# Attention's value products kept in order and side by side, and two 64-row instructions of block 0 widened to 128 rows

## The chip, the cores and the metric

One core of one Trainium2 chip runs the whole program. TensorE (PE in the profile) does the matmuls and transposes, VectorE (DVE) the reductions and part of the copies, ScalarE (ACT) the exponentials and the other copies, GpSimd (POOL) the scaling of probabilities and some subtractions; SyncE (SP) issues the transfers. Each engine runs its instructions in one fixed order and waits on semaphores of the others. The metric is the device time of one execution in microseconds: median 2144.94 of three runs (2144.15 to 2150.67).

## The reference

Attention with a memory read is computed for 4 batches and 8 heads of 576 positions and 64 features, and two feed-forward layers follow. Only attention is touched here.

```python
scores = scale * np.matmul(q, k.transpose(0, 1, 3, 2))
scores = np.where(causal, -1000000000.0, scores)
scores = scores - scores.max(-1, keepdims=True)
a = np.exp(scores)
a /= a.sum(-1, keepdims=True) + 1e-09
local = np.matmul(a, v)
q_p = phi(q)                       # phi(x) = max(x, 0) + exp(min(x, 0))
mem_ret = np.einsum('bhsd,bhde->bhse', q_p, M_prev)
mem_norm = np.einsum('bhsd,bhd->bhs', q_p, z_prev)[..., None] + 1e-06
g = 1.0 / (1.0 + np.exp(-beta))[None, :, None, None]
return (g * mem_ret / mem_norm + (1 - g) * local).astype(np.float32)
```

The result goes through a gated layer (`moe1` in the kernel) and a layer of eight weighted experts (`moe2`).

## The kernel before

Two heads are handled together as a pair; there are 16 pairs. The 576 queries of a head are cut into a first block of 64 (block 0) and four blocks of 128 (blocks 1 to 4). Each pair goes through step sequences, written as Python generators, whose letters stand in three tables (`BEGIN`, `ORDER`, `END`): L loads and splits the inputs, Q prepares phi(q) and its normalizer, S makes the scores and their exponentials, N and K scale the probabilities, V transposes them, W and U multiply them with the values. `ORDER` is one iteration; it is repeated 13 times, each letter taken from the pair that `LAG` gives, so that steps of four neighbouring pairs are interleaved. A scheduler may still move instructions of different steps against each other on each engine; the outcome is a fixed order per engine.

Scores (`scores`, lines 335 to 394). Score tiles `ps` lie in two PSUM buffers that are handed round in turn: block 4 takes both, one for each head (L349, mask L354), then block 3 takes the first one again (L303, 128 x 448), block 2 the second, block 1 the first, block 0 the second (L489, mask L387). A buffer comes free when the exponentials that read it are done: L359 for block 4, one activation for each head, L379 for blocks 3 to 1, L391 for block 0. The exponential needs the row maximum from VectorE first (L358, L375, L389). `QH` and `QL` (L258, L260) are the split queries of a later pair; they have two buffers as well, so `QH` is written when block 0's products (L489, 64 columns), the last to read that buffer, are done.

Transposes (`transposed`, lines 407 to 443). The transposed phi (L414) and probabilities (L424, L432, L441, and L433 for block 0's phi) go to tiles `pt`, three PSUM buffers in turn, and are copied by ScalarE or VectorE into `F`, `T`, `Z` (L398, L403).

Values (`values`, lines 445 to 466). For a pair the output tile `po` collects the memory product (L489, `F`), then for k from 3 to 0 the products of the transposed probabilities `T` with the values (L457): 128, 256, 384 and 512 columns, once for each head. The two heads write the upper and the lower 64 partitions of `po`, so each of these products uses one half of TensorE's columns (the form 128\*64 in the profile, 128\*128 for a full-size instruction and 64\*128 for one that contracts over 64 rows). Every product of plain float32 values is two instructions.

After the 16 pairs `moe1` begins; its weights are unpacked on VectorE (`narrow`, L502 to L507) while its first products run.

Of the kernel before, what the change touches and what calls it, by code (L numbers as in the profile page):

```python
# [12 lines left out]
BF16 = mybir.dt.bfloat16  # L13
# [6 lines left out]
P = 128  # L20
# [20 lines left out]


ORDER = """
    S V L L S Q U V S U V U Q V K U S V S V Q V Q W W V W Q N L V N S V L N V
"""
LAG = {"L": 1, "Q": 0, "S": 0, "N": 0, "K": -1, "V": -1, "W": -1, "U": -2}

# [76 lines left out]
class Kernel:  # L124
# [29 lines left out]

    n_pairs = None

    def attention(self, after=None):
        nc, tc = self.nc, self.tc  # L160
        with ExitStack() as st, ExitStack() as first:
            pool = lambda n, b, to=st, **k: to.enter_context(tc.tile_pool(name=n, bufs=b, reuse_waits="tile", **k))

            self.s1, self.s2 = (pool(f"s{n}", n, first, side="right") for n in (1, 2))
            self.a1, self.a2, self.a3, self.a4 = (pool(f"a{n}", n) for n in (1, 2, 3, 4))
            self.pss = pool("pss", 2, space=PSUM)
            self.pst = pool("pst", 3, space=PSUM)
            self.pso = pool("pso", 1, space=PSUM)
            a1 = self.a1
            self.identb = self.s1.tile([P, P], BF16, name="identb")  # L170
            nc.vector.tensor_copy(self.identb, self.ident)

            self.mask = self.s1.tile([P, P], BF16, name="mask")
            nc.gpsimd.memset(self.mask, 0.0)
            nc.gpsimd.affine_select(
                out=self.mask, in_=self.mask, compare_op=ALU.is_ge, fill=MASKED,
                base=0, pattern=[[1, P]], channel_multiplier=-1,
            )
            self.mask0 = self.s1.tile([64, 2, 64], BF16, name="mask0")
            for j in range(2):  # L180
                nc.vector.tensor_copy(self.mask0[:, j], self.mask[0:64, 0:64])
            busy = self.pso.tile([P, 512], F32, name="po")

            bt = self.s1.tile([P, H], F32, name="bt")
            nc.sync.dma_start(bt, self.beta.partition_broadcast(P))

            eb = self.eb = self.s1.tile([P, H], F32, name="eb")
            nc.scalar.activation(eb, bt, AF.Exp, scale=-1.0)
            nc.vector.tensor_scalar_add(eb, eb, 1.0)
            g1 = self.s1.tile([P, H], F32, name="g1")  # L190
            nc.vector.reciprocal(g1, eb)
            nc.vector.tensor_scalar(g1, g1, -1.0, 1.0, op0=ALU.mult, op1=ALU.add)
            nc.vector.reciprocal(g1, g1)


            self.gs = a1.tile([P, NP, 9], F32, name="gs")
            gv = g1.rearrange("p (a h) -> p a h", h=2)
            for j in range(2):
                nc.vector.tensor_copy(self.gs[64 * j:64 * j + 64, :, 0], gv[64 * j:64 * j + 64, :, j])
                for i in range(4):  # L200
                    nc.vector.tensor_copy(self.gs[:, :, 1 + 2 * i + j], gv[:, :, j])
            wg = self.s1.tile([P, NK, E], F32, name="wg")
            nc.sync.dma_start(wg, self.wg)
            nc.scalar.copy(self.wgs[:, :, 0], wg)
            nc.vector.tensor_sub(self.wgs[:, :, 1], wg, f32(self.wgs[:, :, 0]))

            self.P0 = []
            for n in range(2):
                t = a1.tile([P, 2, D], F32, name=f"P0{n}")
                nc.vector.memset(t, 0.0)  # L210
                self.P0.append(t)

            pairs = [(b, hp) for b in range(B) for hp in range(NP)][:self.n_pairs]
            n = len(pairs)
            live = [dict(b=b, hp=hp, P0=self.P0[hp % 2]) for b, hp in pairs]
            for p in live:
                p["steps"] = {
                    "L": self.load(p), "Q": self.prepare(p), "S": self.scores(p), "N": self.normalize(p),
                    "V": self.transposed(p), "W": self.values(p),
                }  # L220
                p["steps"]["U"], p["steps"]["K"] = p["steps"]["W"], p["steps"]["N"]
            done = object()
            steps = schedule(n)
            for nth, (step, at) in enumerate(steps):
                if nth == len(steps) - len(END.split()) and after:
                    self.ahead = self.load_units()
                    next(self.ahead)
                if step == "X":
                    for _ in range(at):
                        nc.tensor.matmul(busy[:, 0:P], self.mask, self.mask, start=True, stop=True)  # L230
                else:
                    next(live[at]["steps"][step], done)
            first.close()
            if after:
                self.open_early(after)

                with tc.issue_after(self.last_exp.ins):
                    for _ in range(2):
                        next(self.ahead)
                    self.xs = self.split_x(*CHUNKS1[0])  # L240
# [94 lines left out]
    def scores(self, s):  # L335
# [48 lines left out]
        ps = self.pss.tile([P, 2, 512], F32, name="ps")  # L384
        o = ps[:, 0, 0:64]
        self.product(o, cut(q, every, slice(0, P)), cut(k, every, slice(S, S + 64)), True, False)
        nc.tensor.matmul(o, self.mask0.rearrange("k j q -> k (j q)"), self.identb[0:64, 0:64], start=False, stop=True)  # L387
        nm = self.s2.tile([P, 1], F32, name="nm0")
        nc.vector.tensor_reduce(nm, o, axis=AX.X, op=ALU.max, negate=True)  # L389
        for j, h in enumerate(HALVES):  # L390
# [16 lines left out]
    def transposed(self, s):  # L407
        nc, a1, a2 = self.nc, self.a1, self.a2
        phi = s["phi"]

        s["F0"] = F0 = a2.tile([P, 64], F32, name="F0")
        pt = self.pst.tile([P, 512], F32, name="pt")
        for t in range(1, 5):
            nc.tensor.transpose(pt[:, (t - 1) * P:t * P], phi[:, t].rearrange("p j d -> p (j d)"), self.ident)  # L414
        s["F"] = self.split(a2, "F", pt)
        yield

        s["T"] = [self.a4.tile([P, 4, 512], F32, name="T") for j in range(2)]
        for i in range(4, 0, -1):
            for j in range(2):  # L420
                pt = self.pst.tile([P, 512], F32, name="pt")
                for k in range(i):
                    o = (i - 1 - k) * P if j == 0 else 64 + k * P
                    nc.tensor.transpose(pt[:, k * P:(k + 1) * P], s["P"][i][:, j, o:o + P], self.ident)  # L424
                self.copy(
                    8 - 2 * i + j, s["T"][j][:, 0:i, (i - 1) * P:i * P], pt[:, 0:i * P].rearrange("p (k q) -> p k q", k=i)
                )
                yield

        s["Z0"] = Z0 = a1.tile([P, 64], F32, name="Z0")  # L430
        pt = self.pst.tile([P, 512], F32, name="pt")
        nc.tensor.transpose(pt[:, 0:P], s["P0"].rearrange("p j k -> p (j k)"), self.ident)  # L432
        nc.tensor.transpose(pt[:, P:P + 64], phi[0:64, 0].rearrange("p j d -> p (j d)"), self.ident[0:64, 0:64])  # L433
        for h in HALVES:
            self.copy(8, Z0[h], pt[h, h])
        self.copy(8, F0, pt[:, P:P + 64])
        yield
        pt = self.pst.tile([P, 512], F32, name="pt")
        for i in range(1, 5):
            Pi, w = s["P"][i].rearrange("p j k -> p (j k)"), 64 + P * i  # L440
            nc.tensor.transpose(pt[:, (i - 1) * P:i * P], Pi[:, w - 64:w + 64], self.ident)  # L441
        s["Z"] = self.split(a2, "Z", pt)
        yield

    def values(self, s):

        mm, b, T = self.nc.tensor.matmul, s["b"], s["T"]
        x = self.x[:, s["hp"]]
        V0, M = (s["v0m"][:, n * P:n * P + P] for n in range(2))
        po = self.pso.tile([P, 512], F32, name="po")  # L450
        self.product(po, s["MS"], s["F"], True, False)
        yield
        for k in range(3, -1, -1):

            for j, h in enumerate(HALVES):
                v = s["v"][:, 2 * D * k + D * j:2 * D * k + D * j + D]
                mm(po[h, k * P:], v, T[j][:, k, k * P:], start=False, stop=False)  # L457
            yield
        p0 = self.pst.tile([P, 512], F32, name="pt")
        mm(p0[:, 0:64], M, s["F0"], start=True, stop=False)  # L460
        mm(p0[:, 0:64], V0, s["Z0"], start=False, stop=True)
        self.copy(9, x[:, b * S:b * S + 64], p0[:, 0:64])
        yield
        self.product(po, s["V0S"], s["Z"], False, True)
        self.copy(10, x[:, b * S + 64:(b + 1) * S], po)
        yield
# [1025 lines left out]
```

## Time and profile before

| | |
|---|---|
| time of the profiled execution | 2145.09 us |
| its span, first to last instruction | 2143.0 us |
| median of three runs | 2144.94 us |
| TensorE busy, share of the span | 2099.1 us, 98% |
| VectorE, ScalarE, GpSimd busy | 1711.3, 982.6, 530.4 us |
| attention | from the start to about 254 us |
| mean granted TensorE clock | 0.996 |

The profiled execution lies 0.15 us above the median; 2.1 us of it are outside the span. Times in the rows are microseconds from the start of the span. A row of the timeline gives the start, the time until the last of its instructions ends, the engine, the source line, the operation and what it writes and reads; matmuls overlap, so the time that one takes from the engine is read from start to next start. In brackets stands how long the engine sat idle before it and whom it waited for. Rows of windows give the busy time and the number of instructions of each engine, the granted TensorE clock (1.00 is 2.4 GHz, 0.50 is 1.2 GHz) and the transfer rate.

### The profile page before, as it was taken

The page shows a single profiled execution, that of the slowest core. Times are in us where ns is not written, and L with a number is a line of the kernel's source. Part 1 is how long each engine was busy: PE and PEld are TensorE (multiplying, and loading weights), DVE is VectorE, ACT ScalarE, POOL GpSimd, SP SyncE. Part 2 cuts the span into 40 slices and gives each one's busy share as a digit, 9 for nine tenths or more (in the row PEclk, how much of TensorE's full clock was granted, in tenths as well). Part 3 has the DMA queues.
Part 4 walks back from the last instruction along what each step waited for, and adds up shares of the span by engine and source line. Part 5 has one row for each costly group of instructions (what it writes and reads, how often), then busy time and mean ns, then how long its engine had stood idle before and what let it go on. Part 6 is the DMA issues. An engine that isn't in the chain of part 4 may idle for free.

```text
span 2143.0 us, 40649 instructions
## 1 busy us (share of the span) xinstructions
PE 2099.1 (98%) x15848; PEld 1913.9 (89%) x15848; DVE 1711.3 (80%) x3195; ACT 982.6 (46%) x1944; POOL 530.4 (25%) x463
## 2 busy tenths in 40 slices
PE   7999998999999999999999999999999999999999
PEld 5666686878879789999999999999999999999998
DVE  8877798685553676898888889888898888898887
ACT  6888733344332423444444444444444444444442
POOL 7666665000020042121221212212212122121210
PEclk9999999999999999999999999999999999999999
DMA  6322288357567846475565664756647566475564
GB/s 215 126 88 91 91 297 280 136 198 246 191 220 270 284 158 216 160 242 195 192 229 166 236 214 160 246 169 235 213 151 256 182 222 212 160 245 194 194 207 158
DMA packets 123358, 425.76 MB, mean 199 GB/s; under 512 B 13600, under 2 KB 13600, under 8 KB 120096
## 3 DMA queue, kind: packets, MB, share of 16 engines
q1 hardware_dynamic: 123168, 423.17, 58.5%
q8 instruction: 126, 2.06, 0.4%
q14 instruction: 64, 0.52, 0.1%
HBM read 374.36 MB, written 48.76 MB: 197 GB/s over the span
## 4 chain that ended last, share of the span: by engine, by line
PE 75%; DVE 15%; DMA 5%; issue 2%; POOL 2%; ACT 1%; SPq 0%; POOLq 0%; DVEq 0%; ACTq 0%
PE pu L1312 14%; PE pc L1149 13%; PE pq L1312 10%; PE pt L1149 9%; PE po L489 6%; PE pt L1235 4%; PE p L489 4%; DMA xr<-xp 3%; PE pc L489 3%; DVE m L1165 2%; DVE xacc L1318 2%; PE pt L489 2%; PE po L457 2%; PE pq L489 2%; PE pt L424 2%
## 5 line engine op out<-in xcount | busy, mean ns | idle before, releaser
L1312 PE MATMUL pu<-xl,h 128*128 128x256 f32 x3240 | 424.8, 278 | 3.1 <-DVE xacc L1318 2.7
L1149 PE MATMUL pc<-xr,w 128*128 128x256 f32 x3072 | 394.1, 277 | 6.3 <-DMA xr<-xp 4.3
L1312 PEld LDWEIGHTS pu<-xl,h 128*128 128x128 f32 x3240 | 393.1, 188 | 7.6 <-DVE xacc L1318 4.4
L1149 PEld LDWEIGHTS pc<-xr,w 128*128 128x128 f32 x3072 | 370.2, 188 | 9.9 <-issue 5.7
L1312 PE MATMUL pq<-xl,h 128*128 128x256 f32 x2430 | 317.0, 277 | 0.0
L1149 PE MATMUL pt<-xr,w 128*128 128x256 f32 x2304 | 295.0, 277 | 0.1
L1312 PEld LDWEIGHTS pq<-xl,h 128*128 128x128 f32 x2430 | 294.0, 188 | 0.3
L1133 ACT CAST h<-m 128x512 fp32r<-128x512 f32 (+1 forms) x345 | 190.4, 556 | 201.3 <-DVE m L1165 193.6
L1149 PEld LDWEIGHTS pt<-xr,w 128*128 128x128 f32 x2304 | 277.9, 188 | 0.9 <-issue 0.2
L1318 DVE SCALAR_TENSOR_TENSOR xacc<-pu,Pw,xacc 128x256 f32<-128x256 f32 x540 | 237.0, 475 | 39.0 <-PE pu L1312 38.9
L1156 ACT COPY m<-pc 128x512 f32<-128x512 f32 x192 | 111.9, 583 | 252.2 <-PE pc L1149 248.6
L1318 DVE SCALAR_TENSOR_TENSOR xacc<-pq,Pw,xacc 128x256 f32<-128x256 f32 x405 | 177.4, 474 | 47.0 <-PE pq L1312 47.0
L1134 DVE TENSOR_TENSOR h<-m,h 128x512 fp32r<-128x512 f32 (+1 forms) x345 | 207.3, 625 | 1.5
L1055 POOL TENSOR_TENSOR ws<-raw 128x512 f32<-128x512 f32 x62 | 83.7, 1361 | 502.8 <-DMA raw<-w 220.2
L1130 ACT ACTIVATE h<-m 128x512 fp32r<-128x512 f32 x192 | 121.4, 632 | 170.4 <-DVE m L1161 169.3
L1165 DVE SCALAR_TENSOR_TENSOR m<-m 128x512 f32<-128x512 f32 x240 | 186.1, 775 | 14.6 <-ACT m L1192 10.9
L489 PE MATMUL p<-xs,gw 128*128 128x512 f32 (+1 forms) x864 | 173.5, 358 | 6.3 <-DVE hf L674 4.0
L1161 DVE TENSOR_TENSOR m<-pt,m 128x512 f32<-128x512 f32 x192 | 131.2, 683 | 54.1 <-ACT m L1156 52.8
L489 PEld LDWEIGHTS p<-xs,gw 128*128 128x128 f32 x864 | 144.8, 191 | 32.9 <-DVE hf L674 5.6
L1131 DVE SCALAR_TENSOR_TENSOR h<-m,h 128x512 fp32r<-128x512 f32 x192 | 149.1, 777 | 13.0 <-ACT h L1130 12.8
L1042 POOL TENSOR_TENSOR w<-raw,w 128x512 fp32r<-128x512 f32 x17 | 42.1, 2477 | 432.0 <-ACT w L1041 432.0
L489 PE MATMUL po<-h,ws 128*128 128x512 f32 x576 | 144.5, 392 | 2.4 <-ACT h L693 1.2
(244 smaller groups left out, 3015.7 us busy)
## 6 DMA issues: line engine op xcount, KB each, us to landing
xr<-xp SPq DMA_DIRECT2D x480, 512.0 KB, 4.2
raw<-w SPq DMA_DIRECT2D x64, 512.0 KB, 7.4
gw<-kg SPq DMA_DIRECT2D x24, 1024.0 KB, 6.8
graw<-gvo SPq DMA_DIRECT2D x36, 512.0 KB, 5.0
xp<-xl SPq DMA_DIRECT2D x30, 512.0 KB, 4.1
kg<-gw SPq DMA_DIRECT2D x24, 512.0 KB, 4.0
ws<-ko SPq DMA_DIRECT2D x24, 512.0 KB, 3.9
qk<-qkv SPq DMA_DIRECT2D x16, 640.0 KB, 4.2
```

The costliest lines, as they stand in the source:

```text
L489: self.nc.tensor.matmul(out, lhs[a], rhs[b], start=start and n == 0, stop=stop and n == 2, skip_group_check=shared)
L1130: nc.scalar.activation(hi, src, AF.Relu)
L1131: self.later(1, lambda: nc.vector.scalar_tensor_tensor(lo, src, 0.0, f32(hi), op0=ALU.max, op1=ALU.subtract))
L1133: nc.scalar.copy(hi, src)
L1134: self.later(1, lambda: nc.vector.tensor_sub(lo, src, f32(hi)))
L1149: self.marks[3] = nc.tensor.matmul(out[:, j * HT:(j + 1) * HT], w[:, a, j, k], x[:, b, k], start=start and j + k + n == 0, stop=k + n == 3 ...
L1156: self.marks[1] = nc.scalar.copy(t, src)
L1161: nc.vector.tensor_add(t, a, b)
L1165: relu = lambda out, a, b, op: nc.vector.scalar_tensor_tensor(out, a, 0.0, b, op0=ALU.max, op1=op)
L1235: nc.tensor.matmul(ph[:, j * HT:(j + 1) * HT], w[:, b, j, k], x[:, c, k], start=j + a + k + m == 0, stop=a + k + m == 4, skip_group_check= ...
L1312: nc.tensor.matmul(po[:, c], h[a][:, x, j, c * P:(c + 1) * P], w2[b][:, y, j], start=start and c + j + n == 0, stop=j + n == 3, skip_group ...
L1318: self.marks[2] = nc.vector.scalar_tensor_tensor(acc, po[:, c], self.Pw[:, at, e:e + 1], acc, op0=ALU.mult, op1=ALU.add)
```

## The change

The value products of both heads for one k are kept next to each other, and the order in which attention's steps reach TensorE is held: every instruction of a step that is written after a value product is also issued after it on TensorE. In `ORDER` two letters are moved, so that the products for k = 1 and k = 0 stand together, and those for k = 3 and k = 2. Block 0's mask is stored with 128 rows (the lower half zero), and block 0's phi is transposed with 128 rows; both instructions used 64 rows before.

```diff
 ORDER = """
-    S V L L S Q U V S U V U Q V K U S V S V Q V Q W W V W Q N L V N S V L N V
+    S V L L S Q V S U U V U Q V K U S V S V Q V Q W W W V Q N L V N S V L N V
 """
...
-    n_pairs = None
+    n_pairs = last_value = None
...
-            self.mask0 = self.s1.tile([64, 2, 64], BF16, name="mask0")
+            self.mask0 = self.s1.tile([P, 2, 64], BF16, name="mask0")
+            nc.gpsimd.memset(self.mask0, 0.0)
             for j in range(2):
-                nc.vector.tensor_copy(self.mask0[:, j], self.mask[0:64, 0:64])
+                nc.vector.tensor_copy(self.mask0[0:64, j], self.mask[0:64, 0:64])
...
-                    next(live[at]["steps"][step], done)
+                    with ExitStack() as order:
+                        if self.last_value:
+                            order.enter_context(tc.issue_after(self.last_value.ins))
+                        next(live[at]["steps"][step], done)
...
-        nc.tensor.matmul(o, self.mask0.rearrange("k j q -> k (j q)"), self.identb[0:64, 0:64], start=False, stop=True)
+        nc.tensor.matmul(o, self.mask0.rearrange("k j q -> k (j q)"), self.identb[:, 0:64], start=False, stop=True)
...
-        nc.tensor.transpose(pt[:, P:P + 64], phi[0:64, 0].rearrange("p j d -> p (j d)"), self.ident[0:64, 0:64])
+        nc.tensor.transpose(pt[:, P:2 * P], phi[:, 0].rearrange("p j d -> p (j d)"), self.ident)
...
-                mm(po[h, k * P:], v, T[j][:, k, k * P:], start=False, stop=False)
+                self.last_value = mm(po[h, k * P:], v, T[j][:, k, k * P:], start=False, stop=False)
+                self.tc.keep_in_program_order(self.last_value)
```

In the changed file these lines are 4 to 5 further down: the value products L457 are L461 there, the transposes L424 are L428, the products L303, L349 and L489 are L307, L353 and L494, the exponentials L359 are L363, `QH` is L262.

On TensorE, in the middle of one iteration of the steady part, the order before is this (`ps` scores, `pt` transposes, `po` output; L457 with "x2" is both heads, without it one head):

```order
L414 MATMUL pt<-ident,ph 128x128 x4
L457 MATMUL po<-T,vm 64x384 x2
L424 MATMUL pt<-ident,P_1576 128x128 x4
L457 MATMUL po<-T,vm 64x512
L303 MATMUL ps<-KH,QH 128x448 x2
L303 MATMUL ps<-KL,QH 128x448 x2
L303 MATMUL ps<-KH,QL 128x448 x2
L373 LDWEIGHTS mask
L373 MATMUL ps<-identb,mask 128x128
L373 LDWEIGHTS mask
L373 MATMUL ps<-identb,mask 128x128
L457 MATMUL po<-T,vm 64x512
```

And in the changed kernel, at the same place on TensorE:

```order
L418 MATMUL pt<-ident,ph 128x128 x4
L428 MATMUL pt<-ident,P_1577 128x128 x4
L307 MATMUL ps<-KH,QH 128x448 x2
L307 MATMUL ps<-KL,QH 128x448 x2
L307 MATMUL ps<-KH,QL 128x448 x2
L377 LDWEIGHTS mask
L377 MATMUL ps<-identb,mask 128x128
L377 LDWEIGHTS mask
L377 MATMUL ps<-identb,mask 128x128
L461 MATMUL po<-T,vm 64x384 x2
L461 MATMUL po<-T,vm 64x512 x2
```

The 384-column products and one head's 512-column product have moved from ahead of block 3's scores (128x448) to behind them.

At the end of the same iteration TensorE's order before is:

```order
L489 MATMUL po<-F,vmr 128x512 x3
L457 MATMUL po<-T,vm 64x128 x2
L424 MATMUL pt<-ident,P_1700 128x128
L457 MATMUL po<-T,vm 64x256 x2
L424 MATMUL pt<-ident,P_1700 128x128
L489 MATMUL ps<-KH,QH 128x64
```

In the changed kernel TensorE has there:

```order
L494 MATMUL po<-F,vmr 128x512 x3
L461 MATMUL po<-T,vm 64x128 x2
L461 MATMUL po<-T,vm 64x256 x2
L428 MATMUL pt<-ident,P_1701 128x128 x2
L494 MATMUL ps<-KH,QH 128x64
```

One transpose no longer stands between the 128- and the 256-column products.

On ScalarE, from the split of the queries to the exponentials of block 4, the order before is:

```order
L258 ACTIVATE QH<-qk 128x640
L391 ACTIVATE P_176,sums<-ps,nm_1744 64x64 x2
L398 COPY Z_1748<-pt 64x64 x2
L398 COPY F_1596<-pt 128x64
L403 CAST Z<-pt 128x512
L280 ACTIVATE ph<-zq 128x640
L264 CAST KH<-qk 128x640
L403 CAST F<-pt 128x512
L359 ACTIVATE P_1775,sums<-ps,nm_1792 128x576
```

In the changed kernel ScalarE's order over the same stretch is:

```order
L262 ACTIVATE QH<-qk 128x640
L395 ACTIVATE P_177,sums<-ps,nm_1745 64x64 x2
L402 COPY Z_1749<-pt 64x64 x2
L402 COPY F_1597<-pt 128x64
L407 CAST Z<-pt 128x512
L284 ACTIVATE ph<-zq 128x640
L268 CAST KH<-qk 128x640
L407 CAST F<-pt 128x512
L363 ACTIVATE P_1776,sums<-ps,nm_1793 128x576
```

Nothing has moved in this stretch of ScalarE.

## Rows read from the trace of the kernel before

**Rows 1.** Windows, the steady part of attention: busy time by engine, clock, transfers

```profile
80.00:222.00 142.00, 142.00 (x972) 87.39 (x971) 104.75 (x220) 120.82 (x347) 88.41 (x138) 1.00 0.28 89
```

**Rows 2.** Timeline of TensorE, one iteration of the steady part

```profile
150.02 0.44 PE L457 MATMUL po<-T,vm 128*64 128x128 f32 x4
150.39 0.33 PE L424 MATMUL pt<-ident,P 128*128 128x128 f32 x1
150.65 0.65 PE L457 MATMUL po<-T,vm 128*64 128x256 f32 x4
151.23 0.33 PE L424 MATMUL pt<-ident,P 128*128 128x128 f32 x1
...
151.54 0.28 PE L489 MATMUL ps<-KH,QL 128*128 128x64 f32 x1
...
152.34 0.66 PE L441 MATMUL pt<-ident,P 128*128 128x128 f32 x4
...
154.89 0.87 PE L457 MATMUL po<-T,vm 128*64 128x384 f32 x4
155.69 0.66 PE L424 MATMUL pt<-ident,P 128*128 128x128 f32 x4
156.28 1.07 PE L457 MATMUL po<-T,vm 128*64 128x512 f32 x2
157.28 0.47 PE L303 MATMUL ps<-KH,QH 64*128 64x448 f32 x2
...
158.30 1.07 PE L457 MATMUL po<-T,vm 128*64 128x512 f32 x2
159.30 0.66 PE L424 MATMUL pt<-ident,P 128*128 128x128 f32 x4
...
164.38 0.44 PE L457 MATMUL po<-T,vm 128*64 128x128 f32 x4
```

**Rows 3.** Timeline of ScalarE in the same iteration

```profile
151.74 0.74 ACT L258 ACTIVATE QH<-qk 128x640 fp32r<-128x640 f32 x1 [0.72 <-PE ps L489]
...
156.12 0.74 ACT L359 ACTIVATE P<-ps,nm 128x576 f32<-128x576 f32 x1
```

**Rows 4.** Timeline of ScalarE and of TensorE at the start of attention

```profile
15.62 0.74 ACT L359 ACTIVATE P<-ps,nm 128x576 f32<-128x576 f32 x1 [2.73 <-DVE nm L358]
...
16.51 0.47 PE L303 MATMUL ps<-KH,QH 64*128 64x448 f32 x2 [2.38 <-ACT P L359]
```

**Rows 5.** Timeline of TensorE at the end of attention, last pair

```profile
251.12 1.72 PE L457 MATMUL po<-T,vm 128*64 128x384 f32 x8
252.77 0.43 PE L460 MATMUL pt<-F,vm 128*128 128x64 f32 x2
```

**Rows 6.** Timeline of ScalarE, third pair and fifth

```profile
42.87 0.74 ACT L359 ACTIVATE P<-ps,nm 128x576 f32<-128x576 f32 x1
...
79.93 0.74 ACT L258 ACTIVATE QH<-qk 128x640 fp32r<-128x640 f32 x1 [0.25 <-PE ps L489]
```

**Rows 7.** Timeline of TensorE, three waits at and after the end of attention

```profile
245.96 0.74 PE L424 MATMUL pt<-ident,P 128*128 128x128 f32 x5 [2.80 <-DVE xacc L398]
...
340.27 3.02 PE L489 MATMUL p<-xs,gw 128*128 128x512 f32 x12 [2.17 <-DVE sg L674]
...
365.50 10.08 PE L489 MATMUL p<-xs,gw 128*128 128x512 f32 x36 [1.92 <-DVE hf L674]
```

**Rows 8.** Windows behind those waits

```profile
246.00:249.00 3.00, 3.00 (x17) 2.30 (x19) 2.67 (x6) 2.19 (x5) 1.28 (x1) 0.66 0.16 18
249.00:252.00 3.00, 3.00 (x17) 1.34 (x15) 2.06 (x5) 2.01 (x7) 1.94 (x1) 0.77 0.62 244
340.00:360.00 20.00, 19.11 (x81) 15.16 (x82) 19.34 (x34) 8.37 (x15) 8.21 (x5) 1.00 0.83 265
360.00:370.00 10.00, 8.08 (x29) 6.17 (x28) 8.57 (x16) 2.77 (x5) 5.15 (x3) 0.83 0.79 280
```

**Rows 9.** Timeline of TensorE, value products of the last pair in the first of these windows

```profile
248.21 1.55 PE L457 MATMUL po<-T,vm 128*64 128x128 f32 x8
```

## The prediction

> **What bounds the kernel now.** I read the windows of attention first, because the change touches nothing else. Between 80 and 222 us TensorE is busy all the time, ScalarE 120.82 of 142.00 us, VectorE 104.75 and GpSimd 88.41 [rows 1]. That looks like a stage that any relief of TensorE shortens. The timeline then gives one iteration: from one 128-column value product to the next are 164.38 - 150.02 = 14.36 us [rows 2]. Last I looked for the places where TensorE and ScalarE meet, since ScalarE has only some 2.1 us of slack in an iteration (14.36 x 21.18 / 142). Two matter. ScalarE waits 0.72 us before it splits the queries (`QH`, 151.74), for the last product of block 0 that reads the buffer (151.54, row of TensorE) [rows 2, 3]. And TensorE may begin block 3's scores (157.28) only when the first exponential of block 4 (156.12) has freed the score buffer [rows 2, 3]. Where TensorE truly waited for that exponential, its product started 16.51 - 15.62 = 0.89 us after the exponential's start [rows 4]. So at 157.28 the buffer had been free since 156.12 + 0.89 = 157.01: in the steady part that limit is hidden by 0.27 us only. Behind it stands what TensorE does before it, above all the 384-column products and one head's 512-column product.
>
> **The change part by part, TensorE's own work.** A block of value products costs 0.37 us for 128 columns, 0.58 for 256 and 0.80 for 384, both heads together (150.02 to 150.39, 150.65 to 151.23, 154.89 to 155.69) [rows 2]: 0.21 for 128 more columns and about 0.16 for entering and leaving the half-width form. One head's 512 columns alone cost 1.00, and that twice (156.28, 158.30) [rows 2]. 384 and 512 columns of both heads in one block cost 252.77 - 251.12 = 1.65 us [rows 5]. So 0.80 + 1.00 + 1.00 = 2.80 becomes 1.65, and 0.37 + 0.58 = 0.95 becomes 0.79. The transpose between the two small blocks (0.26, 150.39 to 150.65) falls to the pitch of a run, about 0.09; the four transposes behind the 384 columns (0.59, 155.69 to 156.28) lose some 0.1. Block 0's last product, its mask, a transpose and the 64-row transpose take 152.34 - 151.54 = 0.80 now [rows 2]; in one form the four are estimated at 0.4. Together TensorE loses 1.15 + 0.16 + 0.17 + 0.1 + 0.4 = 2.0 us of work in an iteration.
>
> The Trainium skill (TensorEngine Tiling (Array Packing), Tiling Modes, key properties) says that different tiles of the array compute in parallel and that a change of the tiling mode drains it. The trace agrees: two heads' 384 columns take less than one head's 512, and each separate block pays its 0.16 [rows 2]. By that rule alone 13 iterations would give the gain that stands below as the second rival.
>
> **Where the time of an iteration goes then.** In the order of the changed kernel the following chain closes on itself, whatever TensorE has to spare. From `QH` to the first exponential of block 4 ScalarE does the same instructions in the same order as before, without a hole: 156.12 - 151.74 = 4.38 [rows 3]. Then 0.89 to block 3's first product [rows 4], 1.02 to the end of its mask (157.28 to 158.30), the joint block 1.65 [rows 5], the unchanged stretch to the 128-column products, 164.38 - 159.30 = 5.08, from there to block 0's last product 151.54 - 150.02 = 1.52 less 0.16 and 0.17, so 1.19, and 0.20 to the next `QH` [rows 2, 3]. The sum is 14.41 us against 14.36. What was taken from TensorE ahead of block 3's scores is lost there as a wait, and the value products put behind them (1.65 where 1.00 stood) lengthen the chain by what the other end saves. TensorE would reach block 3's scores at about 154.89 + 0.59 - 0.4 = 155.1, and the buffer is free at 157.01: a new wait of some 1.9 us on ScalarE in each iteration. Queued behind it are the value products, the second half of block 4's transposes and the copies of ScalarE that need them. I count 10 such iterations: 10 x 0.05 = +0.5 us. Bounds: -0.1 to +0.2 for each, if the estimated pitch of the transposes or the exponential's release is off by a tenth.
>
> The early pairs. The third pair's exponential starts at 42.87, held by VectorE [rows 6], which unpacks weights there; it is not moved. With the changed order block 3 follows at 42.87 + 0.89 = 43.76, the next `QH` 1.02 + 1.65 + 5.08 + 1.19 + 0.20 = 9.14 later at 52.9, and two more iterations of 14.41 bring it to 81.7, where it stood at 79.93 [rows 6]: +1.8. VectorE has its unpacking between block 3's maximum and block 2's in the new order, which may add up to 1.0. I take +2.3, with bounds of 0 (the unpacking moves out of the way) and +3.
>
> The last pairs keep TensorE's order except for block 0's two widened instructions and the joint small block; ScalarE's copies there wait for block 0's transposes, so about 0.4 is gained: -0.4, bounds -1 and 0.
>
> The memset of the mask on GpSimd and the pins themselves cost nothing: GpSimd waits for the first inputs then, and a pin only fixes the order, which is counted above. The feed-forward layers keep their work; the shift of attention's end passes through to the end, give or take 2 us for the unpacking of weights on VectorE.
>
> **The clock.** TensorE had no idle time in the steady part [rows 1] and the clock held 1.00, its level of 2.4 GHz. A wait of 1.9 us is new. This trace shows what can follow one: after idle 2.80 us (until 245.96) the granted clock of the next stretches is 0.66 and 0.77, a time at the level of 1.2 GHz within them; after 1.92 us (until 365.50) it is 0.83; after 2.17 us (until 340.27) it stays 1.00 [rows 7, 8]. So I expect about half of the 13 waits (third pair to the thirteenth iteration) to be followed by a time at half clock. Its price: 128 and 256 columns together, 0.79 at full clock, took 1.48 there by the start of the next instruction (1.55 to the end) [rows 9], and over both windows 3.00 x 0.34 + 3.00 x 0.23 = 1.7 us of clock are missing [rows 8]. What follows the wait lies on the closed chain with no slack, so nearly all of it counts: I take 1.3 each, 6.5 x 1.3 = +8.5, bounds 0 and 13 x 1.7 = +22.
>
> The Trainium skill (TensorE: Matmul & The Clock Gate, Why this matters for your kernels) advises against idle gaps only when they are longer than this one; by it the clock would hold and the sum would be the first rival's. The trace speaks against it with the wait of 1.92 us [rows 7, 8], and for it with the one of 2.17.
>
> **Sum.** 0.5 + 2.3 - 0.4 + 8.5 = +10.9 us on the profiled execution's 2145.09, which lies 0.15 above the median: 2156 us.
>
> **The rivals.** First, the clock holds: the same closed chain, without the 8.5: 2145.09 + 2.4 = 2147.5, no change that counts. For it speaks the wait of 2.17 us without a fall; against it the other two. Chance 0.28.
>
> Second, not slower but faster: TensorE alone sets the pace, as its 142.00 of 142.00 suggest [rows 1]. Then 13 x 2.0 = 26 us go, to about 2119. Its place is block 3's scores: it decides if the first exponential of block 4 comes 1.9 us sooner after `QH`. Against it: ScalarE's stretch has neither a hole nor a new order. Chance 0.05.
>
> Third, every wait costs the clock, at 1.7: 2145.09 + 2.4 + 22 = 2169.6. For it speaks that most waits of this size in the trace did. Chance 0.10.
>
> Fourth, the layers behind attention take the shift back: TensorE waits for VectorE's unpacked weights there, two of these waits alone 2.17 and 1.92 us [rows 7]; if VectorE gets ahead, some 5 of the 10.9 us return: 2151. Chance 0.08.
>
> That the change does not do what it says: the order shows both heads side by side, but if two heads gained nothing from it the block of 1.65 would be about 3.5 and the time above 2170. The rows exclude nearly all of this; 0.02. The forecast keeps 0.47.
>
> **How the numbers follow.** A measurement of this kernel tells about 0.3%, 6.4 us, from no change: 2138.5 to 2151.4 counts as the same. Slower takes most of the forecast (0.44 of 0.47), the third rival, part of the fourth and the last: 0.58. The same takes the first rival, part of the fourth and what is left of the forecast: 0.36. Faster is the second rival and a little more for the early pairs: 0.06. The range of 8 in 10 runs from 2145, which takes in the first rival, to 2167, which leaves out most of the third. The forecast's own range is 2150 to 2163.
>
> **What would show it.** Right: in the steady part an idle time of TensorE before block 3's scores, put down to the exponential L363, of 1.5 to 2.2 us in nearly every iteration; a period of 14.3 to 14.5 us where the clock is full and about 1.3 longer where it fell; granted clock below 1.00 in several windows of 80 to 222 us; value products of both heads in one block of 1.65 us. Wrong: a period near 12.5 us, no idle time of TensorE there, or a clock of 1.00 throughout.

## The result, and the profile after

The changed kernel took 2157.1 us (median of 5 runs, 2155.0 to 2162.6) against 2144.9 before (5 runs): 1.0057 times, 95% interval 1.0042 to 1.0072. Predicted were 2156 us. The profiled execution is the longest of the five, 2162.6 us with a span of 2160.8; what is read from it below adds up to more than the 12.2 us between the medians.

The windows of the profile show the same stretch as [rows 1]: the window, its length, busy time of TensorE, its weight loads, VectorE, ScalarE and GpSimd, the granted clock, transfers.

```profile
80.00:222.00 142.00, 127.57 (x923) 86.91 (x922) 95.12 (x208) 115.98 (x326) 83.72 (x130) 0.95 0.30 96
```

TensorE, busy all of the 142 us before, now idles 14.4 of them, and the clock fell from 1.00 to 0.95. The table of waits for that stretch has a single entry for TensorE (total, times, longest):

```profile
PE ps L307 <- ACT P L363: 14.4, 9, 1.6
```

Nine waits of 1.6 us at block 3's scores, each for block 4's first exponential. ScalarE's timeline, to be held against [rows 3]:

```profile
87.14 0.27 ACT L402 COPY T<-pt 128x128 f32<-128x128 f32 x1 [0.48 <-PE pt L428]
87.39 0.74 ACT L262 ACTIVATE QH<-qk 128x640 fp32r<-128x640 f32 x1
...
88.45 0.31 ACT L395 ACTIVATE P<-ps,nm 64x64 f32<-64x64 f32 x1
...
91.77 0.74 ACT L363 ACTIVATE P<-ps,nm 128x576 f32<-128x576 f32 x1
...
101.82 0.75 ACT L262 ACTIVATE QH<-qk 128x640 fp32r<-128x640 f32 x1
```

QH to the exponential is 4.38 us as before, and QH to QH 14.43 us where it was 14.36. TensorE in the same iteration, and at the start of block 3 of the next:

```profile
87.19 0.28 PE L494 MATMUL ps<-KH,QL 128*128 128x64 f32 x1
...
88.90 0.40 PE L353 MATMUL ps<-KH,QH 64*128 64x288 f32 x1
...
90.01 0.61 PE L418 MATMUL pt<-ident,ph 128*128 128x128 f32 x4
90.46 0.60 PE L428 MATMUL pt<-ident,P 128*128 128x128 f32 x4
92.66 0.47 PE L307 MATMUL ps<-KH,QH 64*128 64x448 f32 x2 [1.60 <-ACT P L363]
...
93.68 1.72 PE L461 MATMUL po<-T,vm 128*64 128x384 f32 x8
95.33 0.66 PE L428 MATMUL pt<-ident,P 128*128 128x128 f32 x4
...
107.09 0.47 PE L307 MATMUL ps<-KH,QH 64*128 64x448 f32 x2 [1.59 <-ACT P L363]
...
108.11 2.76 PE L461 MATMUL po<-T,vm 128*64 128x384 f32 x8
110.79 1.11 PE L428 MATMUL pt<-ident,P 128*128 128x128 f32 x4
```

The joint block takes 95.33 - 93.68 = 1.65 us, as [rows 5] said. After the wait that ends at 107.09 the same eight products take 2.68 us, behind an equal wait at 92.66 they don't. The windows behind three of the waits, as [rows 8]:

```profile
92.00:96.00 4.00, 3.34 (x23) 1.75 (x23) 2.62 (x5) 2.52 (x7) 1.64 (x2) 1.00 0.33 75
106.00:110.00 4.00, 2.91 (x16) 1.18 (x16) 2.62 (x4) 2.86 (x7) 2.06 (x3) 0.83 0.24 44
...
166.00:170.00 4.00, 3.53 (x14) 1.57 (x16) 2.62 (x4) 2.52 (x7) 1.44 (x1) 0.59 0.38 105
```

From the wait that ends at 60.59 on there are 12 such waits; half clock (1.2 GHz) follows 6 of them (60.59, 76.6, 107.09, 166.5, 182.5, 213.0). An iteration with a fall lasts 16.06 us (101.82 to 117.88), 1.63 more than one without. Only this execution of the five has a trace, so how many falls the median one had isn't known.

The early pairs lost most in one place, between the fourth QH (34.34) and the fifth (55.33), 20.99 us apart where 14.93 stood. TensorE's waits there, and the windows behind the first:

```profile
37.00 1.12 PE L428 MATMUL pt<-ident,P 128*128 128x128 f32 x4 [2.62 <-POOL P L337]
...
43.73 0.74 PE L307 MATMUL ps<-KH,QH 64*128 64x448 f32 x2 [2.20 <-ACT P L363]
```

```profile
38.00:42.00 4.00, 2.96 (x15) 2.30 (x14) 4.00 (x7) 3.60 (x12) 2.88 (x2) 0.50 0.16 23
42.00:46.00 4.00, 2.27 (x10) 1.26 (x12) 3.89 (x8) 1.67 (x4) 3.54 (x7) 0.50 0.57 210
```

Some 10 us are at half clock; what that stretch cost is read at the end of the experiments. The later QH of [rows 6] stands at 87.39 instead of 79.93, +7.5, and the last one at 223.75 instead of 209.19, +14.6. (Called the fifth in the rows' heading and in two expectations, it is the seventh of sixteen; here it is "the QH of [rows 6]".)

### The profile page after: what moved, and what is told of

Its sections match the earlier page's. It is cut to its first block, busy times and chain, and to the rows that moved or that the text cites. A ratio compares the mean times of both kernels' runs of the same rounds, so it can differ in the third digit from the quotient of the medians.

```text
span 2160.8 us, 40647 instructions
## 1 busy us (share of the span) xinstructions
PE 2092.6 (97%) x15848; PEld 1920.8 (89%) x15848; DVE 1709.3 (79%) x3195; ACT 985.3 (46%) x1944; POOL 527.2 (24%) x464
## 4 chain that ended last, share of the span: by engine, by line
PE 76%; DVE 11%; DMA 5%; POOL 3%; issue 2%; ACT 2%; SPq 0%; POOLq 0%; ACTq 0%; DVEq 0%
PE pu L1317 15%; PE pc L1154 13%; PE pq L1317 10%; PE pt L1154 10%; PE po L494 6%; PE pt L1240 4%; PE p L494 4%; DMA xr<-xp 3%; PE pc L494 3%; PE pt L494 2%; PE pq L494 2%; PE po L461 2%; POOL na L523 2%; DVE xacc L1323 2%; DVE m L1170 2%
## 5 line engine op out<-in xcount | busy, mean ns | idle before, releaser
L494 PE MATMUL p<-xs,gw 128*128 128x512 f32 (+1 forms) x864 | 170.9, 354 | 5.1 <-DVE sg L679 2.2
L494 PEld LDWEIGHTS p<-xs,gw 128*128 128x128 f32 x864 | 142.4, 188 | 31.9 <-DVE sg L679 3.5
L494 PE MATMUL po<-h,ws 128*128 128x512 f32 x576 | 146.0, 395 | 2.7 <-ACT h L698 1.5
```

What stands on the lines that cost most here:

```text
L494: self.nc.tensor.matmul(out, lhs[a], rhs[b], start=start and n == 0, stop=stop and n == 2, skip_group_check=shared)
```

## The experiments

Each was timed beside the kernel before on the same chip, whose median was 2146.0 us for experiments 1, 2 and 4, 2144.0 for 3, 5 and 6, and 2145.4 for 7. Ratios are to it. The changed kernel was not timed again beside them; a difference to it in microseconds is between medians of different sessions.

**1. The widening alone, and the change without it.** The first is before with these lines, the second the changed kernel with them undone:

```
-self.mask0 = self.s1.tile([64, 2, 64], BF16, name="mask0")
+self.mask0 = self.s1.tile([P, 2, 64], BF16, name="mask0")
+nc.gpsimd.memset(self.mask0, 0.0)
...
-nc.tensor.transpose(pt[:, P:P + 64], phi[0:64, 0].rearrange("p j d -> p (j d)"), self.ident[0:64, 0:64])
+nc.tensor.transpose(pt[:, P:2 * P], phi[:, 0].rearrange("p j d -> p (j d)"), self.ident)
```

> Before, with only the mask and the phi transposition of block 0 widened to 128 rows; the order of the steps and the scheduling of the value products are those of before. If TensorE's work sets the pace of before, the 0.4 us that the two wide instructions save per pair is time off the path: 13 x 0.4 = 5 us less, 2140 us. If the closed chain through ScalarE is nearly as long as TensorE's work (14.36 us against the chain's 14.09 without the joint block's longer time), a pair shortens by no more than the 0.27 us that are free there: 2.7 to 3.5 us less, 2142 us, and a first short wait on block 4's exponential shows before block 3's scores. Either way the clock stays at 1.00 from 80 to 222 us.

> The changed kernel without the widening: block 0's mask and phi transposition contract over 64 rows again, the order and the pinning stay. If the pace is set by the closed chain through ScalarE, the 0.4 us that TensorE loses again per pair come out of its wait before block 3's scores (1.6 us becomes about 1.2) and the period stays 14.4 us: 2153 to 2158 us, rather less than the changed kernel if a shorter wait costs the clock less often. If TensorE sets the pace: 13 x 0.4 = 5 us more than the changed kernel, 2162 us.

Measured: alone 2144.6 us, 0.9992 (0.9982 to 1.0001); the rest without it 2159.1 us, 1.0053 (1.0035 to 1.0071). Neither differs from its partner. The periods at full clock are their partners' too, 14.36 us and 14.43 us, and the wait without the widening is 1.6 us, not 1.2. For the first run both theories missed: 5 us less lies outside the interval, and 2.7 less, which lies inside it, would need a shorter period. For the second the period stayed as the first theory had it, but the wait did not shrink: the 0.4 us never reached block 3. TensorE's timeline of before, then of the widening alone, shows where they stop:

```profile
151.54 0.28 PE L489 MATMUL ps<-KH,QL 128*128 128x64 f32 x1
...
152.34 0.66 PE L441 MATMUL pt<-ident,P 128*128 128x128 f32 x4
...
153.25 0.40 PE L349 MATMUL ps<-KH,QH 64*128 64x288 f32 x1
...
154.36 0.61 PE L414 MATMUL pt<-ident,ph 128*128 128x128 f32 x4
```

```profile
152.55 0.28 PE L490 MATMUL ps<-KH,QL 128*128 128x64 f32 x1
...
152.96 0.60 PE L442 MATMUL pt<-ident,P 128*128 128x128 f32 x4
...
154.26 0.40 PE L350 MATMUL ps<-KH,QH 64*128 64x288 f32 x1
...
155.38 0.61 PE L415 MATMUL pt<-ident,ph 128*128 128x128 f32 x4
```

The widened instructions save 0.80 - 0.41 = 0.39 us as estimated, but the transpositions behind block 4's scores stand 2.82 and 2.83 us after the same product. QH starts 0.20 behind that product (151.74 and 152.75), and the second head of block 4 begins 1.51 behind QH in before, in the widening alone and in the changed kernel (153.25 - 151.74; 154.26 - 152.75; 88.90 - 87.39). The score buffers are two, so its buffer is the one that block 0 had, and block 0's second exponential (L395, 88.45) stands right before it. In before the two heads' products overlap; with TensorE early, the first head's run alone and the second's come no sooner. Earlier in before, where TensorE had nothing else to do, the profile names this exponential as what the second head waits for (ScalarE, then TensorE):

```profile
38.96 0.31 ACT L391 ACTIVATE P<-ps,nm 64x64 f32<-64x64 f32 x1
```

```profile
39.41 0.39 PE L349 MATMUL ps<-KH,QH 64*128 64x288 f32 x1 [0.18 <-ACT P L391]
```

It starts 0.45 us behind the exponential there, and 0.45 behind it in the three iterations above as well (152.80 to 153.25, 153.81 to 154.26, 88.45 to 88.90). No experiment moved that exponential by itself.

**2. The wait filled with work.** Zeros are added to the open value tile, before block 3's scores of each pair:

```
+for _ in range(26):
+    self.last_value = nc.tensor.matmul(
+        live[at]["po"][:, 0:P], self.zero, self.zero, start=False, stop=False
+    )
+    tc.keep_in_program_order(self.last_value)
```

> The changed kernel with 26 products of a 128x128 tile of zeros before block 3's scores of each pair, accumulated into the value tile that is open there, so that they add zero to it: TensorE works in the stretch in which it waited 1.6 us for block 4's exponential. If the single falls of the clock come from that wait, the granted clock stays at 1.00 from 80 to 222 us, every period there is 14.4 us, and the 6 falls of 1.6 us are gone: 9.6 us less than the changed kernel, 2147 us; with the slow early stretch of 10 us gone too, 2143. The period doesn't fall below 14.4 us, since the chain is as long as it was. If the falls have another cause, or the clock's share of the loss is small, the time stays at 2155 to 2158 us.

Measured: 2148.9 us, 1.0017 (1.0005 to 1.0028), 8.3 less than the changed kernel (8.6 by the ratios). The timeline and the windows of the filled kernel:

```profile
87.80 1.61 PE L240 MATMUL po<-zero 128*128 128x128 bf16 x26
89.58 0.47 PE L316 MATMUL ps<-KH,QH 64*128 64x448 f32 x2 [0.16 <-ACT P L372]
```

```profile
80.00:222.00 142.00, 140.42 (x1226) 102.63 (x1226) 103.35 (x218) 121.40 (x346) 90.59 (x140) 1.00 0.30 94
```

Every period is 14.44 us and the clock holds. So useless work of TensorE bought back two thirds of the loss, and the chain didn't get shorter: the first theory for the steady part. Its second step, the early stretch gone too, did not come: between 20 and 60 us the clock is still 0.84 and 0.88. What is left of the loss lies early: the QH of [rows 6] is at 84.31, still 4.4 us late.

**3. The chain longer.** The cast of Z in four pieces:

```
-self.nc.scalar.copy(t[:, 0], src)
+n = P if name == "Z" else 512
+for c in range(0, 512, n):
+    self.nc.scalar.copy(t[:, 0, c:c + n], src[:, c:c + n])
```

> The changed kernel with ScalarE's cast of Z, which stands between QH and block 4's exponential in its queue, made in four pieces of 128 columns instead of one of 512: four times a pitch of 0.25 us for one of 0.61, so 0.39 us more in the closed chain of a pair, the order of all other work as it was. If ScalarE's queue is the chain that sets the pace, block 4's exponential, TensorE's wait (1.6 becomes 2.0 us) and the period (14.43 becomes 14.82 us where the clock holds) all take the 0.39 us: 13 x 0.39 = 5 us more than the changed kernel, 2162 us, and up to 2172 if the longer wait costs the clock in every pair. If the pace is set elsewhere (the way from block 4's scores through their maximum, or TensorE), the piece is hidden: 2157 us.

Measured: 2165.2 us, 1.0099 (1.0079 to 1.0120). ScalarE and TensorE:

```profile
89.33 0.78 ACT L409 CAST Z<-pt 128x128 fp32r<-128x128 f32 x4
```

```profile
92.76 0.47 PE L307 MATMUL ps<-KH,QH 64*128 64x448 f32 x2 [1.80 <-ACT P L363]
```

The four pieces take 0.78 us where one took 0.59, so the dose was 0.19, not 0.39. It arrived whole: wait 1.60 to 1.80, period 14.43 to 14.63. Of the last 11 periods of QH, 7 have a fall instead of 6. ScalarE's queue is in the chain. The profiled executions differ by 4.3 us, about what 11 periods of 0.20 and one fall more come to (2.2 + 1.6); the medians differ by 8, and that rest isn't explained by these rows.

**4. The chain shorter.** QH, KH and the first phi instruction behind block 4's exponentials:

```
-S V L L S Q V S U U V U Q V K U ...
+S V L S V S U U V Q L U Q V K U ...
...
+if self.block4 and step in "LQ":
+    order.enter_context(tc.issue_after(self.block4.ins))
```

> The changed kernel with ScalarE's QH, KH and first phi instruction of the next pair issued behind block 4's exponentials instead of ahead of them: the closed chain loses 0.65 + 0.61 + 0.65 = 1.9 us. If that chain sets the pace, the wait of 1.6 us before block 3's scores goes, the period falls from 14.4 us towards TensorE's own work of 12.8 us (14.43 less the wait of 1.60), the falls of the clock go with the wait: 13 x 1.2 to 1.6 = 16 to 21 us and some 8 us of clock less, 2128 to 2135 us. If another input is late at once (QL or KL for the next block 4, phi for the transpositions), a new wait of about the same size stands elsewhere: 2145 to 2157 us.

Measured: 2165.4 us, 1.0087 (1.0072 to 1.0102): slower still, the second theory with a price of its own. TensorE, then GpSimd and ScalarE of one iteration:

```profile
168.40 0.40 PE L355 MATMUL ps<-KL,QH 64*128 64x288 f32 x1 [1.23 <-POOL KL L271]
...
171.72 0.47 PE L309 MATMUL ps<-KH,QH 64*128 64x448 f32 x2 [1.09 <-ACT P L365]
```

```profile
166.81 1.53 POOL L271 TENSOR_TENSOR KL<-qk,KH 128x640 fp32r<-128x640 f32 x1
```

```profile
162.31 0.78 ACT L270 CAST KH<-qk 128x640 fp32r<-128x640 f32 x1
```

KH is cast behind block 3's exponentials, GpSimd makes KL of it only at 166.81, behind its normalisations, and the second score product of the next block 4 waits 1.23 us. Block 4's exponential comes later by that (ScalarE's cast of F, next ahead of it, stands idle 2.04 us for TensorE's transpositions) and still holds block 3 for 1.09 us. Period 14.86 us at full clock.

**5. The joint block ahead of block 3's scores.**

```
-S V L L S Q V S U U V U Q V K U ...
+S V L L S Q V U U S V U Q V K U ...
```

> The changed kernel with the joint value block (1.65 to 1.72 us) ahead of block 3's scores instead of behind them; everything else of the change stays. If the loss is the place of that block in the closed chain, it now runs in the wait of 1.60 us for block 4's exponential, and the chain from block 3's scores to the next QH is 1.65 us shorter: the period falls from 14.43 to 12.8 us (14.43 less the wait, TensorE's own work) or at worst 13.4 us if block 3's exponentials free their buffer late, and the clock stays at 1.00. 13 x 1.0 to 1.6 = 13 to 21 us less, and some 8 us of clock less: 2128 to 2136 us. If a wait of the same size comes up at once at block 1's scores, which need the buffer of block 3's exponentials, the period stays near 14.4 us and only the clock is given back or not: 2147 to 2157 us.

Measured: 2137.8 us, 0.9966 (0.9953 to 0.9980), faster than both kernels. TensorE's timeline, and the windows:

```profile
100.25 1.72 PE L461 MATMUL po<-T,vm 128*64 128x384 f32 x8
101.93 0.47 PE L307 MATMUL ps<-KH,QH 64*128 64x448 f32 x2
...
106.67 0.36 PE L307 MATMUL ps<-KH,QH 64*128 64x192 f32 x2 [0.41 <-ACT P L383]
```

```profile
80.00:222.00 142.00, 137.49 (x1049) 95.93 (x1051) 108.67 (x238) 130.10 (x376) 107.87 (x152) 1.00 0.28 93
```

The wait is gone, the block does in it what it did behind it, the period is 13.34 us ((203.26 - 83.21) / 9) and the clock holds. The next wait is the one named beforehand, block 1's scores for block 3's exponentials, at 0.41 us. The time lies 2 us above the range expected; the QH of [rows 6] (83.21), still 3.3 us late, would account for it.

**6. The order of before, with the rest of the change.**

```
-S V L L S Q V S U U V U Q V K U S V S V Q V Q W W W V Q ...
+S V L L S Q U V S U V U Q V K U S V S V Q V Q W W V W Q ...
```

> The changed kernel with the order of before, in which the value products of one k stand apart from those of the next: heads side by side, the pinning and the widening stay. The products of k = 1 (about 0.7 us) then stand ahead of block 3's scores, those of k = 0 behind them, and TensorE changes twice more into the half-column form, 2 x 2 x 0.16 us. If the place of the value products in the closed chain sets the pace, the chain is shorter by 0.7 us and TensorE's work longer by 0.6 us: both come to 13.5 to 13.8 us a pair against 14.43, the wait before block 3's scores falls to 0.2 to 0.4 us and the clock holds: 2157 less 13 x 0.65 less 8 = 2138 to 2143 us. If TensorE's work set the pace of the changed kernel: 8 us more, 2165 us.

Measured: 2149.2 us, 1.0024 (1.0012 to 1.0036).

```profile
92.10 0.47 PE L307 MATMUL ps<-KH,QH 64*128 64x448 f32 x2 [0.66 <-ACT P L363]
```

The mechanism is as expected (shorter wait, clock 1.00 in 80 to 222 us), the size isn't: period 14.09 us. I had left a piece of the chain out. k = 1 taken out shortens it by 1.65 - 1.00, but the small blocks apart and the transpose between them lengthen it by 0.16 + 0.17 [rows 2]: 14.43 - 0.65 + 0.33 = 14.11. The QH of [rows 6] stands at 86.83 here, 6.9 us late, which the expected time left out too.

**7. The first two pairs not pinned,** once on the order of experiment 5, once on the changed kernel:

```
-self.last_value = mm(po[h, k * P:], v, T[j][:, k, k * P:], start=False, stop=False)
-self.tc.keep_in_program_order(self.last_value)
+value = mm(po[h, k * P:], v, T[j][:, k, k * P:], start=False, stop=False)
+if b * NP + s["hp"] >= 2:
+    self.last_value = value
+    self.tc.keep_in_program_order(value)
```

> The kernel with the joint value block ahead of block 3's scores (2137.8 us), in which the value products of the first two pairs are not pinned, those of pair 2 and later are. If the pinning is what makes the early pairs late, TensorE's order there is again nearly that of before, the 5th QH starts at 80 to 81 us instead of 83.2, and the time is 2 to 4 us less: 2134 to 2136 us. If the early pairs are late for the order of the steps or the place of the joint block, the time stays at 2138 us.

> The changed kernel in which the value products of the first two pairs are not pinned, those of pair 2 and later are. If the pinning is what costs the 7.5 us by which the changed kernel's 5th QH is late (87.39 against 79.93 us), most of that comes back: 5th QH at 80 to 82 us, 2150 to 2152 us. If the wait before block 3's scores or the order of the steps makes the early pairs late, the time stays at 2157 us.

Measured: 2134.8 us, 0.9951 (0.9937 to 0.9964), and 2155.5 us, 1.0045 (1.0030 to 1.0059). Both intervals overlap those of the kernels they start from. The first time falls into the range of the first theory, but its QH of [rows 6] (84.03) is as late as without the edit, so the mechanism isn't that theory's. In the second the fifth pair's QH is on time again (50.37 against 50.30), but the sixth comes at 71.78 instead of 65.88: the loss moved by one pair, and the QH of [rows 6] is at 83.71. Its waits of TensorE:

```profile
37.34 0.66 PE L428 MATMUL pt<-ident,P 128*128 128x128 f32 x4 [2.48 <-POOL P L337]
...
53.77 0.30 PE L418 MATMUL pt<-ident,ph 128*128 128x128 f32 x1 [1.80 <-DVE nm L393]
```

So the pins of the first pairs are not the cause.

For what delays the early pairs the traces point to VectorE's unpacking, though no run tried it by itself. In the changed kernel block 3 begins at 43.73, as predicted, but the next QH comes 11.60 us later (55.33), not 9.14. VectorE in before, then VectorE and TensorE in the changed kernel:

```profile
47.15 0.74 DVE L398 COPY T<-pt 128x256 f32<-128x256 f32 x2
...
48.12 0.68 DVE L506 SCALAR_TENSOR_TENSOR nb<-graw,nb 128x512 f32<-128x512 uint32 x1
```

```profile
51.68 1.14 DVE L511 SCALAR_TENSOR_TENSOR nb<-graw,nb 128x512 f32<-128x512 uint32 x1
52.86 1.01 DVE L512 TENSOR_TENSOR nb<-na,nb 128x512 f32<-128x512 f32 x1
...
54.26 0.74 DVE L402 COPY T<-pt 128x256 f32<-128x256 f32 x2
```

```profile
54.82 0.30 PE L428 MATMUL pt<-ident,P 128*128 128x128 f32 x1 [0.65 <-DVE T L402]
```

The copies into T, ahead of the unpacking in before, now stand behind it, and TensorE waits for them. The half clock ahead of that wait seems to have cost little: VectorE was busy 16.98 of the 18 us from 36 to 54, and in the filled kernel, where the clock is back at 1.00 from 46 us on, TensorE waits 1.56 us for the same copies and the QH comes at 55.45. Experiments 5 and 6 show waits for VectorE's T in the same place, 2.64 us (until 52.62) and 2.27 (until 56.12).

## Why the prediction was right, step by step

- **The closed chain: right.** 14.41 us were predicted, 14.43 measured, and QH to exponential 4.38 as before. One link is another than was named: QH now follows ScalarE's copy of T without idle time (87.14, which waited for a transposition), and still starts 0.20 behind block 0's last product. Experiments 2, 3 and 5 show it: filling the wait leaves the period, a longer queue of ScalarE lengthens it by all of the 0.19, and the joint block taken out of the chain shortens it by 1.09.
- **TensorE's work: one term failed.** "Block 0's last product, its mask, a transpose and the 64-row transpose ... in one form the four are estimated at 0.4" was right as work and wrong as arrival: nothing of it passes block 4's second head (experiment 1). The wait is therefore 1.60 us and not 1.9; 1.9 - 0.4 = 1.5, and phi's four transpositions gained the other 0.1 (0.45 instead of 0.53). I had taken block 4's scores for a fixed length.
- **The early pairs: too small.** The term was +2.3: 1.8 for the chain and 0.5 for VectorE's unpacking. The chain's part came (block 3 at 43.73 against 43.76, two periods of 14.43 in the filled kernel); VectorE's was 2.4 (55.33 against 52.9), 2.6 in the filled kernel. With the wait filled the QH of [rows 6] is 4.4 us late, and the profiled execution had 3.1 of clock on top of that, from two falls.
- **The clock: right in kind, each fall dearer.** Half of the waits were to be followed by half clock: 6 of 12 were. The price is 1.63 us, not 1.3, near the upper bound of 1.7. In total 8.5 us were predicted; filling the waits gives back 2157.1 - 2148.9 = 8.3, while six falls of 1.63 would be 9.8 in the profiled execution. The Trainium skill (TensorE: Matmul & The Clock Gate, Why this matters for your kernels) advises in that section against longer gaps only; here gaps of 1.6 us were followed by half clock, so the measurement decides against reading it as a licence.
- **The last pairs: wrong sign, small.** Between the last QH and the end of attention the profiled execution lost another 1.0 us instead of gaining 0.4, with a wait of 3.88 us for VectorE where 2.80 stood [rows 7]. That wait comes with the widening, from which the gain was to come: it is 3.89 with the widening alone and 2.81 in the change without it. Why isn't shown.
- **The rivals.** TensorE alone as the bound (2119) would need a period near 12.5 us: refuted. The clock holding (2147.5) is what experiment 2 built by hand for the steady part: 2148.9. Every wait costing the clock: 6 of 12 didn't. The layers behind attention gave nothing back: the profiled execution is 15.6 us late at their first product (269.61 against 254.02) and 17.8 at the end of its span.

That 2156 met 2157 to a microsecond is in part luck. In the only execution that has a trace nearly every term came out larger than predicted: the early pairs' order 4.2, six falls 9.8, the steady chain 0.6, the last pairs 1.0 and the layers behind 2.2, together 17.8 us against the 10.9 of the forecast. The median execution, 5.5 us faster than this one, lies near the forecast; which of the terms is smaller there isn't shown.

## What to carry to other kernels

An engine that is busy 100% of a stretch need not set its pace: add up the closed chain through the other engines first, since work taken from the busy engine ahead of a point where the chain joins it only becomes a wait there. When such a wait appears, move work that already exists into it, from behind the point to ahead of it; here that turned +0.57% into -0.34%. Look too at what the new order puts ahead of the copies on another engine: here it was unpacking for a later layer. And a wait of TensorE has two prices, its own length on the chain and the clock behind it.

## What the runs showed of the hardware

- Equal waits had unequal ends. After 1.60 us the clock fell in 6 of 11 periods (5 of 11 in the change without the widening), after 1.80 in 7 of 11; with the waits at 0.16, 0.41 and 0.66 us (experiments 2, 5 and 6) it read 1.00 over 80 to 222 us. Short waits can be followed by half clock too: in the first run of experiment 7 waits of 0.24, 0.21 and 0.59 us (until 80.09, 82.79 and 84.20) were followed by half clock from 86 to 92 us. The stretch at half clock that followed the early waits lasted some 10 us, those in the steady part cost 1.6 us each.
- Score products of two heads on 64 rows each overlap only when both may run: the twelve of 288 columns and two masks took 1.43 us in before (152.93 to 154.36) and 1.89 where the first head came early and the second didn't (153.49 to 155.38).
- A cast of 128x512 cut into four on ScalarE costs 0.19 us more (0.78 against 0.59).
